# Re-ordering the first chunk of a fused LayerNorm, linear attention and gated-MLP kernel: half-chunk first units, K inside gate/up, LayerNorm further ahead, weight loads in thirds

## Chip, cores, metric

The kernel runs on one core of a Trainium2 chip. The metric is the device time of one execution in microseconds (us), lower is better. A time is a median of several executions; the span in a profile is about 1.7 us shorter than the time of that same execution (566.5 and 568.19 us before, 536.1 and 537.85 changed).

## The reference

One block of a model, on 2048 tokens of width 576 in bf16. A LayerNorm feeds two branches that are added to the input: linear attention with 32 heads of 18, and a gated MLP of width 4608.

```python
xn = layernorm(x)                                  # x: 1 x 2048 x 576
q, k, v = heads(xn @ wqkv)
pq, pk = phi(q), phi(k)                            # phi(t) = (t + 1 if t > 0 else exp(t)) + 1e-6
kv = einsum("bhsd,bhse->bhde", pk, v);  z = sum_s pk
attn = (pq @ kv / (pq . z + 1e-6)) @ wo
mlp = (sigmoid(xn @ w_gate) * (xn @ w_up)) @ w_down
out = x + attn + mlp
```

## The kernel before

Tokens are worked on in 16 tiles of 128 and in 4 chunks of 512 (four tiles). What matters here:

- *GU(c, f)*: one of 36 gate/up units of a chunk: 9 x 2 matmuls of 64 rows, the upper and the lower half of the array at the same time, into a pair of accumulator banks. Then tanh on ScalarE and one VectorE operation that writes hT.
- *K(t)*: the K projection of two tiles, one in each half of the array; it takes two pairs of banks. *K1(t)* is the same for one tile. Its output goes through exp (ScalarE) and two VectorE operations into pk.
- *L1, L2, L3a, L3b, TD*: LayerNorm statistics (VectorE), small powers and products (POOL), normalisation (ScalarE for tiles 4 and up), then the transposed copy xs by two DMA transposes per tile, issued on SP's queue.
- *Q*: query projections. *G*: products xn by pk over all 16 tiles. They need all of K. *den*: denominators, whose reciprocals take VectorE 3.3 us each.
- *ring*: three weight slots of four units each, gate in partitions 0 to 63, up in 64 to 127.
- *pair()* hands out one of four pairs of banks.

A small scheduler derives semaphore waits from the named tiles; each engine executes its instructions in program order. The start and the first chunk are:

```python
TP(0) ...                                  # tiles 0-3: transposed on TensorE
K1(0); TP(2) ...; K1(1); TP(3) ...; K1(2); K1(3)
LNx(4)                                     # normalise and transpose tiles 4, 5
ring_load(1, sp)                           # slot 1, issued behind those transposes
f = 0
for p, nf in enumerate((5, 3, 3, 3, 2, 2)):
    ta = 6 + 2 * p
    for n in range(nf):
        GU(0, f); f += 1
        ...                                # statistics of ta, ta+1; LNx(ta); x loads; slot 2
    K(4 + 2 * p)                           # needs the transposes issued one round before
...                                        # [cut: Q, G(4), z]
G(0); dq = den(0, (0, 1)); G(1)
for fn in dq: fn()                         # two reciprocals at once
...                                        # [cut: same for den 2, 3 and 4; rest of gate/up with Q]
attn(0, a0); finish(0, a0)
for fn in dq: fn()                         # two reciprocals ahead of ...
attn(1, a1); finish(1, a1)                 # ... what frees the accumulator
```

## Time and profile before

| | before |
|---|---|
| median time | 569.01 us (568.57 to 569.63, 3 runs) |
| span of the profiled run | 566.5 us |
| first Q unit, which needs all K, begins | 97.53 us |
| chunk 0 ends (chunk 1's gate/up begins) | 228.69 us |
| chunks 1 and 2 | 112.14 us each |

These are lines of the profile page: the engines' busy time (part 1), and the granted clock in 40 slices of 14 us, in tenths (part 2).

```profile
PE 525.4 (93%) x4615; PEld 318.1 (56%) x4615; DVE 258.7 (46%) x365; ACT 128.4 (23%) x212; POOL 36.0 (6%) x65
...
PEclk9969797998999979999999999999999999999999
```

TensorE is 93% busy, but the clock line shows that part of that is at a lower clock, always in the first 16 slices (the granted clock was 0.50, half, from 32 to 40 us). The next lines are from the view of waits, TensorE alone: who waited for whom, us in total, times, longest.

```profile
PE ps L478 <- DMA xs<-wd: 10.9, 3, 5.5
PE ps L513 <- DMA ring<-in_B_w_gate_dram: 9.2, 1, 9.2
PE ps L532 <- DVE ost L707: 7.4, 3, 6.4
...
PE ps L492 <- DVE den L541: 2.5, 1, 2.5
```

The first two are waits for transposed tiles and for weights, the last two for a VectorE that is busy with reciprocals. All but 1 us of these four waits lie before 229 us.

### The profile page before, as it was taken

Reading aid. Unit: us, or ns where it says so; the run is one execution under the profiler, and the core shown is the slowest. Engines: PE = TensorE matmul, PEld = TensorE weight load, DVE = VectorE, ACT = ScalarE, POOL = GpSimd, SP = SyncE. Lnnn points to the kernel's source line nnn. Section 1 sums busy time; section 2 is a strip of 40 time slices with the busy share of each in tenths; the row PEclk is TensorE's granted clock in tenths of the full one; section 3 lists DMA queues with packets and bytes.
Section 4 is the critical chain, followed back from the end, with each engine's and each line's share of the span. In section 5 each row is a group of like instructions: output and inputs, shape, how many; then the busy total and the mean of one; then the engine's idle time right before and its main releaser. Section 6 shows DMA issues by size and latency. Waiting matters only on the chain.

```text
span 566.5 us, 10534 instructions
## 1 busy us (share of the span) xinstructions
PE 525.4 (93%) x4615; PEld 318.1 (56%) x4615; DVE 258.7 (46%) x365; ACT 128.4 (23%) x212; POOL 36.0 (6%) x65
## 2 busy tenths in 40 slices
PE   7739668998999959999999999999999999999997
PEld 3416457864546737444447774444477744444776
DVE  5606362798642097233338903333388033333001
ACT  4504233312432100232230002232200022233000
POOL 3504242300000000000000000000000000000000
PEclk9969797998999979999999999999999999999999
DMA  9299984428848010277774103667831047760000
GB/s 248 58 216 229 150 166 89 119 61 254 195 101 184 6 42 22 61 145 153 168 162 91 43 22 83 146 141 155 168 84 43 23 100 146 148 130 1 22 22 21
DMA packets 72999, 62.54 MB, mean 110 GB/s; under 512 B 17786, under 2 KB 72954, under 8 KB 72954
## 3 DMA queue, kind: packets, MB, share of 16 engines
q1 hardware_dynamic: 52202, 41.08, 32.0%
q10 hardware_dynamic: 20752, 20.79, 18.1%
q8 instruction: 36, 0.59, 0.5%
q14 instruction: 9, 0.07, 0.1%
HBM read 55.97 MB, written 2.36 MB: 103 GB/s over the span
## 4 chain that ended last, share of the span: by engine, by line
PE 82%; DVE 9%; DMA 5%; issue 1%; ACT 1%; POOL 1%; SPq 1%; DVEq 0%; ACTq 0%
PE ps L513 47%; PE ps L693 22%; DVE den L549 5%; PE ps L492 4%; PE ps L701 3%; PE ps L478 3%; PE ps L560 2%; DMA xs<-wd 2%; DMA ring<-in_B_w_up_dram 2%; DVE den L541 1%; DMA pqT<-in_A_x_dram 1%; PE ps L532 1%; PE ps L467 1%; DVE stats L387 1%; DVE ost L707 1%
## 5 line engine op out<-in xcount | busy, mean ns | idle before, releaser
L513 PE MATMUL ps<-xs,ring 64*128 64x512 bf16 x2592 | 286.6, 378 | 11.5 <-DMA ring<-in_B_w_gate_dram 9.2
L513 PEld LDWEIGHTS ps<-xs,ring 64*128 64x128 bf16 x2592 | 133.9, 95 | 159.6 <-issue 15.2
L521 DVE SCALAR_TENSOR_TENSOR hT<-tg,ps 128x512 bf16<-128x512 f32 x144 | 98.9, 687 | 167.9 <-PE ps L513 143.9
L519 ACT ACTIVATE tg<-ps 128x512 f32<-128x512 f32 x144 | 85.9, 597 | 320.8 <-PE ps L513 303.2
L693 PE MATMUL ps<-wd,hT 128*128 128x288 bf16 x1152 | 147.1, 287 | 0.0
L693 PEld LDWEIGHTS ps<-wd,hT 128*128 128x128 bf16 x1152 | 112.9, 98 | 32.1 <-issue 2.2
L549 DVE RECIPROCAL den<-den 126x512 f32<-126x512 f32 (+1 forms) x20 | 66.9, 3343 | 0.0
L707 DVE SCALAR_TENSOR_TENSOR ost<-ps,xr 128x576 bf16<-128x576 f32 x16 | 12.1, 756 | 78.7 <-PE ps L701 72.7
L478 PE MATMUL ps<-hT,xs 64*128 64x288 bf16 x216 | 19.7, 335 | 11.9 <-DMA xs<-wd 10.9
L452 DVE TENSOR_SCALAR et<-et 128x576 bf16<-128x576 bf16 (+2 forms) x36 | 11.9, 331 | 34.1 <-ACT et L451 34.1
L451 ACT ACTIVATE et<-ps 128x576 bf16<-128x576 f32 (+2 forms) x36 | 20.6, 616 | 30.3 <-PE ps L492 16.4
L492 PE MATMUL ps<-xs,wqM 64*126 64x512 bf16 (+1 forms) x180 | 22.4, 397 | 2.5 <-DVE den L541 2.5
L478 PEld LDWEIGHTS ps<-hT,xs 64*128 64x128 bf16 x216 | 15.0, 110 | 16.2 <-issue 10.9
L701 PE MATMUL ps<-wqM,pqT 126*128 126x288 bf16 (+1 forms) x160 | 22.1, 286 | 0.0
L460 POOL TENSOR_TENSOR hT<-hT,wd 128x576 f32<-128x576 f32 x15 | 19.2, 1281 | 38.3 <-DVE wd L453 37.7
L492 PEld LDWEIGHTS ps<-xs,wqM 64*126 64x126 bf16 (+1 forms) x180 | 14.7, 137 | 9.1 <-DVE den L541 3.0
L541 DVE TENSOR_SCALAR den<-ps 126x512 f32<-126x512 f32 (+1 forms) x20 | 13.0, 684 | 14.8 <-PE ps L532 14.8
L701 PEld LDWEIGHTS ps<-wqM,pqT 126*128 126x128 bf16 (+1 forms) x160 | 15.6, 98 | 4.0
L560 PE MATMUL ps<-wd 128*128 128x288 bf16 x128 | 16.3, 286 | 0.0
L387 DVE BATCH_NORM_STATS2 stats<-pqT 128x6 f32<-128x288 bf16 x32 | 14.6, 456 | 3.7 <-DMA pqT<-in_A_x_dram 3.2
L560 PEld LDWEIGHTS ps<-wd 128*128 128x128 bf16 x128 | 12.4, 98 | 3.5
L550 DVE TENSOR_TENSOR pqT<-pqT,den 126x512 bf16<-126x512 bf16 (+1 forms) x20 | 13.8, 691 | 0.7
(49 smaller groups left out, 117.5 us busy)
## 6 DMA issues: line engine op xcount, KB each, us to landing
ring<-in_B_w_gate_dram SPq DMA_DIRECT2D x36, 576.0 KB, 5.6
ring<-in_B_w_up_dram ACTq DMA_DIRECT2D x33, 576.0 KB, 7.9
wd<-in_B_w_down_dram SPq DMA_DIRECT2D x2, 1296.0 KB, 6.5
wd<-in_B_w_down_dram SPq DMA_DIRECT2D x2, 1152.0 KB, 7.2
xr<-in_A_x_dram SPq DMA_DIRECT2D x16, 144.0 KB, 2.3
out_dram<-ost SPq DMA_DIRECT2D x16, 144.0 KB, 1.8
ring<-in_B_w_up_dram SPq DMA_DIRECT2D x3, 576.0 KB, 9.9
hT<-in_A_wqkv_dram ACTq DMA_DIRECT2D x2, 576.0 KB, 6.5
```

The lines of the kernel that those rows point to most:

```text
L387: V(lambda e, h=h: e.bn_stats(stats_t[:, so + 6 * h:so + 6 * h + 6], x_in(t, 288 * h, 288)), reads=["x[%d]" % t], writes=["st%d" % (t % 4)])
L451: A(lambda e: e.activation(e3, src, AF.Exp), reads=kb, writes=["et%d" % j])
L460: P(lambda e: e.tensor_tensor(zacc, zacc, pk(tt, 0, _D), ALU.add), reads=["pk[%d]" % tt, "zacc"], writes=["zacc"])
L478: T(lambda e, s=s, h=h, p0=p0, tt=tt, b=b: e.matmul(bank(b + h, 128, 0, 288), xs(s, 128 * tt, 128, p0, p0 + 64), wk(s, 288 * h, 288, p0, p ...
L492: T(lambda e, k=k, half=half, c=c, i=i, g=g, sl=sl, p0=p0: e.matmul(bank(b + half, g, 0, _CH), wq(k, i, half, g), xs(sl, _CH * c, _CH, p0, ...
L513: T(lambda e, k=k, half=half, sl=sl, p0=p0: e.matmul(bank(b + half), ring(r, k, fo, half), xs(sl, _CH * c, _CH, p0, p0 + 64), start=(k == ...
L519: A(lambda e: e.activation(tg, bank(b), AF.Tanh, scale=0.5), reads=["pb%d" % b], writes=["tg%d" % sj])
L521: V(lambda e: e.scalar_tensor_tensor(hT(f), tg, 1.0, bank(b + 1), ALU.add, ALU.mult), reads=["pb%d" % (b + 1), "tg%d" % sj], writes=["hT[% ...
L549: V(lambda e: e.reciprocal(dn(j, g), dn(j, g)), reads=["dn%d" % j], writes=["dn%d" % j])
L560: T(lambda e, t=t, h=h: e.matmul(bank(b + h, 128, 0, 288), xn(t, 128 * j, 128), pk(t, 288 * h, 288), start=(t == 0), stop=(t == NT - 1)), ...
L693: T(lambda e, f=f, h=h: e.matmul(bank(acc + h, 128, 0, 288), hT(f, 128 * st, 128), wd(f, h), start=(f == 0), stop=False), reads=["hT[%d]" ...
L701: T(lambda e, i=i, g=g, h=h: e.matmul(bank(acc + h, 128, 0, 288), pqT(i, 128 * t, 128, g), M(i, h, g), start=False, stop=(i == _NG - 1)), ...
```

## The change

The intent is to give TensorE gate/up work as soon as two tiles are transposed, to keep K out of the start, to have LayerNorm's output ready earlier, and to remove the waits for reciprocals. Its core, cut:

```diff
+        x_load(1, 2, (), act)
+        x_load(2, 4)
+        ring_mixed(0, act)              # slot 0 before the K weights, in thirds of 192 KB
 ...
+        ring_mixed(1)                   # slots 1 and 2 at the start, thirds gate/up alternating
+        ring_mixed(2)
 ...
+        GU_mm(0, 0, b0, 0, 256)         # units 0 and 1 on tiles 0 and 1
+        GU_mm(0, 1, b1, 0, 256)
 ...                                     # tiles 2 and 3
+        GU_mm(0, 0, b0, 256, 256); GU_out(0, 0, b0)
+        GU_mm(0, 1, b1, 256, 256); GU_out(0, 1, b1)
 ...
-        for p, nf in enumerate((5, 3, 3, 3, 2, 2)):
+        late = {4: lambda: (x_load(8, 12), ring_mixed(3)), 6: lambda: x_load(12, 16), 8: lambda: ring_mixed(4),
+                10: wq_load, 12: lambda: ring_mixed(5)}
+        kt = {3: 0, 5: 2, 8: 4, 10: 6, 12: 8, 14: 10, 16: 12, 17: 14}
+        for f in range(2, FK):
+            GU(0, f)
+            ta = f + 2 - f % 2
+            if f < 14:
+                if f % 2 == 0: LNa(ta)                 # statistics
+                else: LNb(ta); late.get(ta, ...)()     # normalise, transpose; loads
+            if f in kt: K(kt[f])
 ...
-        G(0); dq = den(0, (0, 1)); G(1); (both reciprocals)
+        dq = den(0, (0, 1)); G(0); dq[0](); G(1); dq[1]()
 ...
-                for fn in dq:
-                    fn()
                 attn(1, a1)
                 finish(1, a1)
+                for fn in dq:
+                    fn()
 ...
-  plan = {0: [(8, (0, 1)), (24, (2, 3))], 1: [(8, (4,))]}
+  plan = {0: [(8, (0, 1))], 1: [(8, (2, 3))], 2: [(8, (4,))]}
```

Cut here: `pair()` now gives the pair that was given or released longest ago, tiles 1 and 3 are partly copied out by VectorE, and the loads of w_down are spread over units 19 to 25. The four K1 become two K, and the dummy matmuls (`warm`) at the start are placed differently. `plan` says in which tile of the down projection, and after how many of its steps, the dens of the next chunk are placed.

More of the change, by code (lines that the diff above doesn't have):

```diff
@@ L223, in bass_parallel_sum__linear_attn_block__glu_gated_glu__prompt_kernel, with release @@
         held = set()
-        turn = [0]
+        order = [0, 1, 2, 3]
         def pair():
-            while True:
-                p = turn[0] % 4
-                turn[0] += 1
-                if p not in held:
-                    return 2 * p
+            p = next(q for q in order if q not in held)
+            order.remove(p)
+            order.append(p)
+            return 2 * p
+        def release(b):
+            p = b // 2
+            held.discard(p)
+            order.remove(p)
+            order.append(p)
         def xs(slot, c0, n, p0=0, p1=128):
@@ L300, in ring, with x_load @@
             return ring_t[64 * half:64 * half + 64, o:o + 128]
-        def x_load(ta, tb, extra=()):
+        def x_load(ta, tb, extra=(), q=None):
             dst = pqT_t[:, ta * _D:tb * _D].rearrange("p (t d) -> p t d", t=tb - ta)
-            load("x%d" % ta, dst, xv[:, ta:tb, :], ["x[%d]" % t for t in range(ta, tb)], None, extra)
+            load("x%d" % ta, dst, xv[:, ta:tb, :], ["x[%d]" % t for t in range(ta, tb)], q, extra)
         wg_v = B_w_gate.rearrange("(k p) f -> p k f", p=64)
@@ L307, in bass_parallel_sum__linear_attn_block__glu_gated_glu__prompt_kernel, with ring_part @@
         wu_v = B_w_up.rearrange("(k p) f -> p k f", p=64)
-        ringL_p = [dprod("rl%d" % r) for r in range(R)]
-        ringU_p = [dprod("ru%d" % r) for r in range(R)]
+        KP = ((0, 3), (3, 6), (6, 9))
+        ringL_p = [[dprod("rl%d%d" % (r, n)) for n in range(3)] for r in range(R)]
+        ringU_p = [[dprod("ru%d%d" % (r, n)) for n in range(3)] for r in range(R)]
         WS = 128 * _FS
-        def ring_load(u, qu=None, extra=()):
+        def ring_part(u, up, n0, n1, q, extra=()):
@@ L313, in ring_load @@
             r = u % R
             j = u % NSLOT
-            dl = ring_t[0:64, r * 9 * WS:(r + 1) * 9 * WS].rearrange("p (k w) -> p k w", k=9)
-            du = ring_t[64:128, r * 9 * WS:(r + 1) * 9 * WS].rearrange("p (k w) -> p k w", k=9)
-            sl = wg_v[:, :, j * WS:(j + 1) * WS]
-            su = wu_v[:, :, j * WS:(j + 1) * WS]
-            sch.dma(sp, ringL_p[r], lambda e: e.dma_start(dl, sl), writes=["ringL[%d]" % r], extra=extra)
-            sch.dma(qu or act, ringU_p[r], lambda e: e.dma_start(du, su), writes=["ringU[%d]" % r], extra=extra)
+            k0, k1 = KP[n0][0], KP[n1 - 1][1]
@@ new lines, in ring_part, with ring_load @@
+            p0 = 64 if up else 0
+            dst = ring_t[p0:p0 + 64, (r * 9 + k0) * WS:(r * 9 + k1) * WS].rearrange("p (k w) -> p k w", k=k1 - k0)
+            src = (wu_v if up else wg_v)[:, k0:k1, j * WS:(j + 1) * WS]
+            name = "ringU" if up else "ringL"
+            sch.dma(q, (ringU_p if up else ringL_p)[r][n0], lambda e: e.dma_start(dst, src),
+                    writes=["%s[%d]%d" % (name, r, n) for n in range(n0, n1)], extra=extra)
+        def ring_load(u):
+            ring_part(u, 0, 0, 3, sp)
+            ring_part(u, 1, 0, 3, act)
@@ L322, in bass_parallel_sum__linear_attn_block__glu_gated_glu__prompt_kernel, with ring_mixed @@
+        def ring_mixed(u, qu=None, extra=()):
+            for n in range(3):
+                ring_part(u, 0, n, n + 1, sp, extra)
+                ring_part(u, 1, n, n + 1, qu or sp, extra)
         x_load(0, 1)
+        x_load(1, 2, (), act)
+        x_load(2, 4)
+        ring_mixed(0, act)
         wkv = A_wqkv[:, _KOFF:_KOFF + _D]
@@ L332, in bass_parallel_sum__linear_attn_block__glu_gated_glu__prompt_kernel @@
         load("wk3", wk_dst(5, 4), wkv[64:576, :].rearrange("(k p) c -> p k c", p=128), ["wk3"], act)
-        x_load(1, 2)
-        x_load(2, 4)
         x_load(4, 6)
-        ring_load(0, sp)
         x_load(6, 8)
+        ring_mixed(1)
+        ring_mixed(2)
         def wq_load():
@@ L358, in bass_parallel_sum__linear_attn_block__glu_gated_glu__prompt_kernel, with wd_load @@
         _nwd = [0]
-        def wd_load(f0, f1, alias=()):
+        def wd_load(f0, f1, extra=()):
             pr = dprod("wd%d" % _nwd[0])
@@ L364, in wd_load @@
             src = B_w_down[f0 * 128:f1 * 128, :].rearrange("(f p) c -> p f c", p=128)
-            sch.dma(sp, pr, lambda e: e.dma_start(dst, src), writes=["wdf[%d]" % f for f in range(f0, f1)] + list(alias))
+            sch.dma(sp, pr, lambda e: e.dma_start(dst, src), writes=["wdf[%d]" % f for f in range(f0, f1)], extra=extra)
         P = lambda fn, reads=(), writes=(): sch.op(pool, fn, reads, writes)
@@ L420, in bass_parallel_sum__linear_attn_block__glu_gated_glu__prompt_kernel, with TP @@
         xs3 = xs_t[:, :].rearrange("p (s c) -> p s c", c=S)
-        def TP(t):
+        def TP(t, ea, eb):
             b = pair()
-            for s in (0, 1, 2, 3, 5, 6, 7, 8, 4):
+            for s in (5, 6, 7, 8, 0, 1, 2, 3, 4):
                 c0 = 128 * s if s < 5 else 64 + 128 * (s - 5)
@@ L429, in TP @@
                   reads=["xn[%d]" % t] + (["xw[%d]" % t] if s == 4 else []) + ["ident"], writes=["pb%d" % bb])
-            A(lambda e: e.activation(xs3[:, 0:5, 128 * t:128 * t + 128], bank_bf(b, 640).rearrange("p (s c) -> p s c", c=128), AF.Identity),
-              reads=["pb%d" % b], writes=["xsA[%d]" % t])
-            A(lambda e: e.activation(xs3[:, 5:9, 128 * t:128 * t + 128], bank_bf(b + 1, 512).rearrange("p (s c) -> p s c", c=128), AF.Identity),
-              reads=["pb%d" % (b + 1)], writes=["xsB[%d]" % t])
+            for st, bb, s0, n, nm in ((eb, b + 1, 5, 4, "xsB[%d]"), (ea, b, 0, 5, "xsA[%d]")):
+                dst, src = xs3[:, s0:s0 + n, 128 * t:128 * t + 128], bank_bf(bb, 128 * n).rearrange("p (s c) -> p s c", c=128)
+                if st is act:
+                    A(lambda e, dst=dst, src=src: e.activation(dst, src, AF.Identity), reads=["pb%d" % bb], writes=[nm % t])
+                else:
+                    V(lambda e, dst=dst, src=src: e.tensor_copy(dst, src), reads=["pb%d" % bb], writes=[nm % t])
         def TD(t):
@@ L460, in K_out @@
                 P(lambda e: e.tensor_tensor(zacc, zacc, pk(tt, 0, _D), ALU.add), reads=["pk[%d]" % tt, "zacc"], writes=["zacc"])
-        def K1(t):
-            b = pair()
-            for s in range(5):
-                rows = 128 if s < 4 else 64
-                for h in range(2):
-                    T(lambda e, s=s, h=h, rows=rows: e.matmul(bank(b + h, 128, 0, 288), xs(s, 128 * t, 128, 0, rows), wk(s, 288 * h, 288, 0, rows),
-                                                              start=(s == 0), stop=(s == 4)),
-                      reads=["xsA[%d]" % t] + (["wk0"] if s < 4 else ["wk1"]), writes=["pb%d" % (b + h)])
-            K_out(t, b)
         def K(t):
@@ L501, in bass_parallel_sum__linear_attn_block__glu_gated_glu__prompt_kernel, with GU_mm @@
         endA = [[]]
-        def GU(c, f):
-            u = c * NSLOT + f // _FS
-            r = u % R
+        def GU_mm(c, f, b, c0, n):
+            r = (c * NSLOT + f // _FS) % R
             fo = (f % _FS) * 128
-            b = pair()
-            xr_ = xsr(range(c * TPC, (c + 1) * TPC))
+            t0 = (_CH * c + c0) // 128
+            xr_ = xsr(range(t0, t0 + n // 128))
             for k in range(9):
@@ L513, in GU, with GU_out @@
                     T(lambda e, k=k, half=half, sl=sl, p0=p0: e.matmul(
-                        bank(b + half), ring(r, k, fo, half), xs(sl, _CH * c, _CH, p0, p0 + 64),
+                        bank(b + half, 128, c0, n), ring(r, k, fo, half), xs(sl, _CH * c + c0, n, p0, p0 + 64),
                         start=(k == 0), stop=(k == 8), tile_position=(p0, 0)),
-                      reads=[("ringU[%d]" if half else "ringL[%d]") % r] + xr_, writes=["pb%d" % (b + half)])
+                      reads=[("ringU[%d]%d" if half else "ringL[%d]%d") % (r, k // 3)] + xr_, writes=["pb%d" % (b + half)])
+        def GU_out(c, f, b):
+            u = c * NSLOT + f // _FS
             sj = f % 2
@@ L522, in GU @@
               reads=["pb%d" % (b + 1), "tg%d" % sj], writes=["hT[%d]" % f] + al)
+            if c == 0 and f < FK:
+                return
             if f % _FS == _FS - 1 and u + R < NUSE:
                 ring_load(u + R)
+        def GU(c, f):
+            b = pair()
+            GU_mm(c, f, b, 0, _CH)
+            GU_out(c, f, b)
         _jd = [0]
@@ L573, in G @@
                       reads=["pb%d" % (b + h)], writes=["GT[4]"])
+        m3 = lambda t_: t_[0:_GW, 0:_GW].rearrange("p (b r) -> p b r", r=_DH)
         warm(11, 7)
@@ L577, in bass_parallel_sum__linear_attn_block__glu_gated_glu__prompt_kernel @@
         L2(0, 1)
-        L1(1, (0,))
+        L1(1)
+        L2(1, 1)
         L3v(0)
-        m3 = lambda t_: t_[0:_GW, 0:_GW].rearrange("p (b r) -> p b r", r=_DH)
-        TP(0)
-        L1(1, (1, 2))
-        L2(1, 1)
+        TP(0, act, act)
         L1(2, (0,))
         L3v(1)
-        warm(3, 7)
-        TP(1)
+        warm(1, 7)
+        TP(1, dve, act)
         L1(2, (1, 2))
         L2(2, 1)
-        L1(3, (0,))
-        L3v(2)
-        K1(0)
-        TP(2)
-        L1(3, (1, 2))
-        L2(3, 1)
-        L1(4)
-        L3v(3)
-        K1(1)
-        TP(3)
+        b0, b1 = pair(), pair()
+        warm(2, 7)
+        GU_mm(0, 0, b0, 0, 256)
+        GU_mm(0, 1, b1, 0, 256)
+        L1(3)
+        L2(3, 1)
+        L3v(2)
+        TP(2, act, act)
+        L3v(3)
+        TP(3, dve, act)
+        GU_mm(0, 0, b0, 256, 256)
+        GU_out(0, 0, b0)
+        GU_mm(0, 1, b1, 256, 256)
+        GU_out(0, 1, b1)
         P(lambda e: e.affine_select(m3(mtmp_t), m3(ones_t), pattern=[[-_DH, 7], [0, _DH]], compare_op=ALU.is_ge,
@@ L603, in bass_parallel_sum__linear_attn_block__glu_gated_glu__prompt_kernel, with LNa, LNb @@
                                     fill=0.0, base=_DH - 1, channel_multiplier=-1), reads=["mtmp"], writes=["mask"])
-        L1(5)
-        L2(4, 2)
-        L3a(4, 2)
-        K1(2)
-        K1(3)
-        def LNx(ta):
+        def LNa(ta):
+            L1(ta)
+            L1(ta + 1)
+            L2(ta, 2)
+            L3a(ta, 2)
+        def LNb(ta):
             for t in (ta, ta + 1):
@@ L613, in LNx @@
                 TD(t)
-        LNx(4)
-        ring_load(1, sp)
-        f = 0
-        for p, nf in enumerate((5, 3, 3, 3, 2, 2)):
-            ta = 6 + 2 * p
-            for n in range(nf):
-                GU(0, f)
-                f += 1
-                if n == 0 and p < 2:
-                    x_load(8 + 4 * p, 12 + 4 * p, paced())
-                if ta < NT:
-                    if n == 0:
-                        L1(ta)
-                    if n == 1:
-                        L1(ta + 1)
-                        L2(ta, 2)
-                        L3a(ta, 2)
-                        if nf == 2:
-                            LNx(ta)
-                    if n == 2:
-                        LNx(ta)
-                if p == 0 and n == 2:
-                    ring_load(2, sp, paced())
-                if p == 2 and n == 0:
-                    wq_load()
-            K(4 + 2 * p)
+        late = {4: lambda: (x_load(8, 12), ring_mixed(3)), 6: lambda: x_load(12, 16), 8: lambda: ring_mixed(4),
[5 more added lines that the diff above has]
+            if f < 14:
+                if f % 2 == 0:
+                    LNa(ta)
+                else:
+                    LNb(ta)
+                    late.get(ta, lambda: None)()
+            if f in kt:
+                K(kt[f])
         wv_load()
         wd_load(34, NF)
+        ring_mixed(6)
         Q(((0, 0), (0, 2)))
@@ L659, in bass_parallel_sum__linear_attn_block__glu_gated_glu__prompt_kernel @@
               reads=["pb%d" % zb, "mask"], writes=["Zx[%d]" % i])
+        dq = den(0, (0, 1))
         G(0)
-        dq = den(0, (0, 1))
+        dq[0]()
         G(1)
-        for fn in dq:
-            fn()
+        dq[1]()
         dq = den(0, (2, 3))
         G(2)
-        for fn in dq:
-            fn()
+        dq[0]()
+        G(3)
+        dq[1]()
         dq = den(0, (4,))
-        G(3)
-        for (f0, f1) in ((0, 9), (9, 18), (18, 26), (26, 34)):
-            wd_load(f0, f1, ["pk[%d]" % t for t in range(NT)] + ["xn[%d]" % t for t in range(NT)] + ["xw[%d]" % t for t in range(NT)])
+        free = paced()
+        wds = [(0, 9), (9, 18), (18, 26), (26, 34)]
         qs = [((1, 0), (1, 2)), ((1, 1), (1, 3)), ((2, 0), (2, 2)), ((2, 1), (2, 3)), ((2, 4), (3, 4)), ((3, 0), (3, 2)), ((3, 1), (3, 3))]
@@ L676, in bass_parallel_sum__linear_attn_block__glu_gated_glu__prompt_kernel @@
             GU(0, f)
-            if dq:
-                dq.pop(0)()
-            elif qs:
+            if f % 2 == 1 and wds:
+                wd_load(*wds.pop(0), extra=free)
+            if f == FK + 1:
+                dq[0]()
+            if f >= FK + 3 and f % 2 == 1 and qs:
                 Q(qs.pop(0))
@@ L710, in finish @@
             sch.dma(sp, out_p[j], lambda e: e.dma_start(out2d[128 * t:128 * t + 128, :], ost_t[:, j * _D:(j + 1) * _D]), reads=["ost%d" % j])
-            held.discard(acc // 2)
+            release(acc)
             if t + 2 < NT:
@@ L772, in bass_parallel_sum__linear_attn_block__glu_gated_glu__prompt_kernel @@
                 finish(0, a0)
+                attn(1, a1)
+                finish(1, a1)
                 for fn in dq:
                     fn()
-                attn(1, a1)
-                finish(1, a1)
                 tiles = (2, 3)
-                plan = {2: [(8, (2, 3)), (24, (4,))]}
+                plan = {2: [(24, (2, 3))], 3: [(24, (4,))]}
             else:
@@ L782, in bass_parallel_sum__linear_attn_block__glu_gated_glu__prompt_kernel @@
                 tiles = range(TPC)
-                plan = {0: [(8, (0, 1)), (24, (2, 3))], 1: [(8, (4,))]} if c + 1 < NCH else {}
+                plan = {0: [(8, (0, 1))], 1: [(8, (2, 3))], 2: [(8, (4,))]} if c + 1 < NCH else {}
             for st in tiles:
```

## The prediction

> **What bounds the kernel now.** I read the chain of work that ended last first. It is 82% TensorE, but the rest is what a reordering can win, so I read the chain in order of time. Three gaps carry most of it: weights (27.87), transposed tiles (57.45 and 81.03), and reciprocals (199.25).
>
> ```profile
> 18.09 4.76 PE ps L513 x44
> 25.80 1.27 SPq L439
> 27.87 9.93 DMA ring<-in_B_w_up_dram
> 37.94 3.45 PE ps L513 x17
> ...
> 57.45 5.76 DMA xs<-wd
> 63.34 4.48 PE ps L478 x35
> ...
> 81.03 5.49 DMA xs<-wd
> 86.77 4.47 PE ps L478 x35
> ```
>
> L513 is gate/up (GU), L478 a pair of K projections. Columns are start, length and what. The first line below, from the timeline of the same stretch, is K with a warm clock: 2.44 us busy, 2.2 from start to the next group, against 4.48 above. The others, from the chain restricted to the end of chunk 0, are the reciprocals.
>
> ```profile
> 73.61 2.47 PE L478 MATMUL ps<-hT,xs 64*128 64x288 bf16 x36
> ...
> 199.25 3.27 DVE den L549
> 202.52 0.02 issue
> 202.54 0.69 DVE pqT L550
> 203.24 3.27 DVE den L549
> 206.51 0.02 issue
> 206.53 0.03 DVE pqT L550
> 206.56 0.57 issue
> 207.14 0.76 DVE ost L707
> 207.90 0.04 issue
> 207.94 1.11 PE ps L532 x2
> ```
>
> Then the table by stretches (PE, PEld, DVE, ACT, POOL, clock, DMA share, GB/s).
>
> ```profile
> 30.00:40.00 10.00, 2.65 (x11) 0.96 (x13) 0.00 (x0) 0.00 (x0) 0.00 (x0) 0.53 1.15 235
> 60.00:70.00 10.00, 7.05 (x57) 5.24 (x59) 1.60 (x4) 2.89 (x5) 1.54 (x6) 0.66 0.94 164
> 80.00:90.00 10.00, 3.51 (x29) 2.51 (x31) 3.65 (x10) 2.17 (x3) 3.50 (x7) 0.76 1.00 183
> 260.00:566.00 306.00, 302.28 (x2650) 177.19 (x2646) 118.57 (x135) 55.49 (x93) 0.00 (x0) 1.00 0.43 93
> ```
>
> After 260 us TensorE is busy 302 of 306 us: nothing is left there. Chunks 1 to 3 cost 112.14 us each (starts 228.69, 340.82, 452.96). All that can be won lies before 228.7. From the chain, with a full clock, one GU is 1.945 us (180 matmuls in 19.43 are ten of them), a K pair 2.19, a tile of the down projection 8.82 plus 1.23 for attention. Chunk 0 holds 36 GU (70.0), K (17.5 as eight pairs), 10 Q units (19.4), G (18.0), four down tiles (40.2) and about 5 of small things: 170 us. It takes 228.7, so some 58 us are start, waits and half clock.
>
> **What the Trainium skill says.** "TensorE: Matmul & The Clock Gate", Part 1 (the HAM clock gate): the array falls to half clock after an idle window of some microseconds and needs a busy one to recover. The trace agrees: clock 0.53 after the 10 us wait, and K at 4.48 instead of 2.2. A removed wait therefore returns more than itself. The same page's specification table calls the ScalarE and VectorE queues strict FIFO; the trace agrees at 207.14, where the cheap ost operation, needed to free the accumulator, stands behind two reciprocals. "DMA: Bandwidth & Descriptors", Issuing engines are not separate DMA queues: splitting loads over SP and ACT saves issue time, not bandwidth. The trace agrees: with both queues loaded, 30 to 36 us shows a DMA share of 1.1 and only 217 to 223 GB/s.
>
> **The change, part by part.** I place the start of the first Q unit, 97.53 us now.
>
> (1) Start. x tiles 0 to 3 and weight slot 0 go first, so tiles 0 and 1 are transposed by 9 us (today TP0 starts at 6.73 and TP1 at 8.56, plus evacuation). Bytes by then: x 0.59 MB and slot 0 1.18 MB, which at the 283 to 383 GB/s of 2 to 8 us takes 6 us from about 2 us on, with some competition from wk. Two half units run from 9.5 to 11.5 (9 x 2 x 256 columns are half of 1.945 each). Tiles 2 and 3 come at 14, because VectorE does two statistics blocks, a copy and two normalisations between. Then the other halves (to 16), units 2 and 3 (19.9), K(0) at about 20. Today GU begins at 17.7 and stalls from 25.9 to 37.9.
>
> (2) Weights. Bytes still to load after slot 0 are wk rest 1.1, x4 to x7 0.59, slots 1 and 2 2.36: 4.05 MB at 225 GB/s is 18 us, done at 27.5. Slot 1 is needed at 22, with thirds arriving first; slot 2 after 30. The 12 us weight stall goes.
>
> (3) Steady stretch. From f=2 to f=17 TensorE wants 16 x 1.945 + 8 x 2.19 = 48.6 us, so from 16.0 the bare end is 64.7. That is 33 us better than 97.5, but the other engines bind. VectorE per two GU, one K pair and one LayerNorm pair is 2 x 0.60 + 2 x 1.02 + (4 x 0.48 + 2 x 0.21 + 0.18) = 5.8 us against TensorE's 6.08. Worse, there is a loop in program order: statistics on VectorE, then 1.57 to L3b's start (49.92 to 51.49 now, through POOL), L3b 1.62 on ACT, tanh 0.60 behind it, hT 0.60, then the next statistics, 2.3. That sums to 6.7 us. In the two rounds where K's exp also sits in that loop it is nearly 9. Rounds of 8.9, 8.8, 6.6, 6.7 and 6.7 carry the statistics of pair 4 (19.4) to those of pair 14 at 57.2; three more K pairs and the remaining GU then end at 74, not 64.7.
>
> (4) SP's queue. It issues, in order, 24 DMA transposes, 18 thirds, x and wq between pairs. Transposes take 1.25 us to issue when quiet, but 4.61, 2.17, 2.23 and 1.27 behind a weight backlog at 29 us. I estimate six pairs at 7.2, 7.8, 5.5, 6.3, 5.9, 6.5 = 39 us, 18 thirds at 0.45 (less than the 0.65 of a whole half slot) = 8, x and wq 3.6. From 25 us that is 76, and with the 4.2 median to landing K(14) can begin near 79 if it never waits for input, 75 if contention is mild. K(14) cold costs 2.2 more. So Q begins between 74 and 84; I take 79.5. That is 18 us won here of 33.
>
> (5) Q to the end of chunk 0's GU (97.53 to 176.21 = 78.7 now). Needed: 3 Q 5.83, G(4) 2.3, z 0.55, five den 1.1, four G 15.7, 18 GU and 7 Q 48.6 = 74.1. The wait of TensorE for den (2.50 at 127) and the half-clock unit after it (3.70 for 1.94) go, since reciprocals are spread. New: the first den now stands before G(0), so it waits for Zx, which today ended its first two pieces about 1.1 us after the z matmuls. 75.2, so 3.5 won.
>
> (6) The down tail of chunk 0 (52.5 now). finish(1) moves ahead of its reciprocals: the 6.37 us wait for ost and the slow matmuls after it (5.19 for 32, against 3.92) go. 8.3 won, 44.2 remain. VectorE has 8 us reciprocals during the next tile, which takes 10 us: they fit.
>
> (7) Chunks 1 and 2: each shows one 0.5 us wait for ost at the last den. Spreading over three tiles wins about 1.5 in all.
>
> Sum: 79.5 + 75.2 + 44.2 + (566.5 - 228.7 - 1.5 = 336.3) = 535.2 of span. Times are 2.5 above the span now (569.01 to 566.5), so 537.7; I say 538.
>
> **Rivals.** (a) *TensorE bound throughout*: the LayerNorm loop is absorbed by the four accumulator pairs. Then Q starts at 65 to 67 and the time is 523 to 526. For it: three rounds at 6.7 are only 10% over 6.08. Against: a K pair needs two accumulator pairs at once, so the slack is about one GU. (b) *ACT/VectorE loop binds, SP doesn't*: Q at 74, time 532. For it: SP issues at 1.25 quiet. (c) *SP's transposes take the place of the weight wait*: Q at 84 with K(14) cold, time 542 or a little more. For it: 29 to 40 us now; against: less weight traffic coincides with the later pairs. (d) *Early weights come late*: the backlog of ring thirds delays wk or slot 1 by 3 to 6 us. This adds only in part, because pair 4's loop starts after K(0): 540 to 545. (e) No gain, as the removed wait reappears in full: I see no mechanism, since 12 us of (6) and (5) don't touch LayerNorm at all.
>
> **Range and chances.** (b), (c) and their middle take most of the weight; (a) perhaps 12%, (d) or something unseen 12%. I put 538 with 528 to 547. Faster by over 2% means under 557.6: that needs only (5), (6) and a small half of (3), so 0.97.
>
> **What would show it.** Q's first matmul (today's L492) at 75 to 84; gate/up starting at 9 to 11 and no long wait for ring; DMA xs<-wd still a wait ahead of the last K pairs if (c), waits of K and GU on hT or pk (VectorE) if (b), and none if (a). In SP's own queue, transposes of 1.2 to 2.3 us, issued nearly back to back. Chunk 0's tail near 44 us with no wait on ost; chunks of 111.4. VectorE over 80% busy from 20 to 60 us. I am wrong if Q starts outside 72 to 86, if GU's start slips beyond 13 us because slot 0 lands late, or if the reciprocals moved behind finish(1) come back as a wait at the start of chunk 1.

## The result

The changed kernel takes 537.97 us (median of 4, 537.76 to 539.44) against 568.94 for the kernel before in the same rounds. The ratio is 0.946, with a 95% interval of 0.944 to 0.948. Ratios here are the mean time of one kernel's fast runs over that of the other's in the same rounds, so not quite the ratio of the medians. Later runs used other rounds, where the kernel before had medians of 566.6 to 568.1 us, so experiments are compared by their ratio to it and by the times inside their traces.

The same lines of the page, changed kernel:

```profile
PE 518.2 (97%) x4683; PEld 317.0 (59%) x4683; DVE 259.5 (48%) x367; ACT 126.0 (24%) x210; POOL 35.8 (7%) x65
...
PEclk9998989999999999999999999999999999999999
```

TensorE does nearly the same work in 7 us less busy time. Less of it is at half clock: the mean granted clock was 0.970 before and is 0.994 now; two slices still dip, to 8. (Line numbers moved: L522 is now gate/up, L488 K, L502 Q, L551 den, L707 the down projection, L721 the last sum.) TensorE's waits in the changed kernel:

```profile
PE ps L488 <- DMA xs<-wd: 3.9, 3, 1.6
PE ps L488 <- DVE wd L473: 3.1, 4, 1.3
...
PE ps L522 <- DVE wd L473: 1.4, 1, 1.4
...
PE ps L551 <- DVE Zexp L670: 1.0, 1, 1.0
```

The wait for weights (9.2 and 2.3 us before) is gone, so are the waits for ost and for reciprocals. What is left is three short waits for transposes, waits for VectorE to empty K's accumulators (pk lies in wd), and the wait for Zx that the prediction had announced. By stages, with the prediction beside it:

| stage | before | predicted | measured |
|---|---|---|---|
| start to first Q | 97.5 | 79.5 | 80.0 |
| Q to the end of chunk 0's gate/up | 78.7 | 75.2 | 75.6 |
| down projection of chunk 0 | 52.5 | 44.2 | 44.1 |
| the rest | 337.8 | 336.3 | 336.3 |
| span | 566.5 | 535.2 | 536.1 |

The loop that the prediction names is seen in VectorE's and ScalarE's timelines. In one round, after statistics that began at 36.77: normalisation, then tanh behind it, then hT, then the next statistics (start, us, operation):

```profile
40.63 1.62 ACT L434 ACTIVATE wd<-pqT,nm,rs 128x576 bf16<-128x576 bf16 x2 [5.01 <-POOL nm L430]
...
42.16 0.57 ACT L531 ACTIVATE tg<-ps 128x512 f32<-128x512 f32 x1
...
42.77 0.69 DVE L533 SCALAR_TENSOR_TENSOR hT<-tg,ps 128x512 bf16<-128x512 f32 x1 [2.94 <-ACT tg L531]
...
43.37 0.95 DVE L405 BATCH_NORM_STATS2 stats<-pqT 128x6 f32<-128x288 bf16 x2
```

In the down tail of chunk 0, the den that stood 6.37 us before now follows without a gap in the chain, after a piece that ends at 184.88:

```profile
184.88 0.43 PE ps L551 x2
185.31 2.94 PE ps L707 x24
```

The chain of waits in time order just before Q shows what set its start:

```profile
63.43 5.54 DMA xs<-wd
...
69.22 2.29 PE ps L488 x34
...
73.93 2.35 DMA xs<-wd
...
76.52 3.70 PE ps L488 x34
```

K(12) waits for the transposes of tile 13, then K(14) for those of tile 15, and K(14) runs near half clock (granted 0.58), 3.70 us where K(12) took 2.29. In SP's queue at that time (start, us, operation):

```profile
64.75 0.60 SPq L326 DMA_DIRECT2D ring<-in_B_w_gate_dram  x1
...
68.89 0.61 SPq L326 DMA_DIRECT2D ring<-in_B_w_up_dram  x1
69.62 1.21 SPq L458 DMA_TRANSPOSE xs<-wd  x1
...
73.93 1.20 SPq L459 DMA_TRANSPOSE xs<-wd  x1
```

The six thirds of weight slot 5 stand ahead of the last transposes. They were issued from 64.75 to 69.50; slot 5 is first used by unit 20, which starts at about 111 us, some 40 us later. The transposes behind them took only 1.20 to 1.27 us each to issue, so it was the place in the queue that held them here.

### The profile page after: what moved, and what is told of

Its sections match the earlier page's. It is cut to its first block, busy times and chain, and to the rows that moved or that the text cites. A ratio compares the mean times of both kernels' runs of the same rounds, so it can differ in the third digit from the quotient of the medians.

```text
span 536.1 us, 10699 instructions
## 1 busy us (share of the span) xinstructions
PE 518.2 (97%) x4683; PEld 317.0 (59%) x4683; DVE 259.5 (48%) x367; ACT 126.0 (24%) x210; POOL 35.8 (7%) x65
## 3 DMA queue, kind: packets, MB, share of 16 engines
q10 hardware_dynamic: 19152, 19.17, 17.5%
## 4 chain that ended last, share of the span: by engine, by line
PE 90%; DVE 4%; DMA 3%; SPq 1%; ACT 1%; issue 1%; POOL 0%; DVEq 0%; ACTq 0%
PE ps L522 50%; PE ps L707 26%; PE ps L715 4%; PE ps L488 3%; PE ps L579 3%; PE ps L502 3%; DMA xs<-wd 1%; DMA ring<-in_B_w_gate_dram 1%; DVE wd L473 1%; PE ps L551 1%; DVE et L472 1%; DVE pqT L473 1%; DVE stats L405 1%; SPq L458 0%; DVE hT L533 0%
## 5 line engine op out<-in xcount | busy, mean ns | idle before, releaser
L522 PE MATMUL ps<-xs,ring 64*128 64x512 bf16 (+1 forms) x2628 | 285.9, 373 | 4.1 <-DVE wd L473 1.4
L522 PEld LDWEIGHTS ps<-xs,ring 64*128 64x128 bf16 x2628 | 134.9, 94 | 150.1 <-DVE xs L453 1.9
L707 PE MATMUL ps<-wd,hT 128*128 128x288 bf16 x1152 | 145.8, 286 | 0.0
L707 PEld LDWEIGHTS ps<-wd,hT 128*128 128x128 bf16 x1152 | 112.2, 98 | 31.2 <-issue 1.7
L721 DVE SCALAR_TENSOR_TENSOR ost<-ps,xr 128x576 bf16<-128x576 f32 x16 | 12.1, 758 | 73.6 <-PE ps L715 54.9
L488 PE MATMUL ps<-hT,xs 64*128 64x288 bf16 x288 | 23.3, 308 | 7.0 <-DMA xs<-wd 3.9
L488 PEld LDWEIGHTS ps<-hT,xs 64*128 64x128 bf16 x288 | 17.0, 102 | 13.3 <-DVE wd L473 3.5
L502 PE MATMUL ps<-xs,wqM 64*126 64x512 bf16 (+1 forms) x180 | 20.8, 376 | 0.0
L502 PEld LDWEIGHTS ps<-xs,wqM 64*126 64x126 bf16 (+1 forms) x180 | 14.1, 128 | 5.5
L579 PEld LDWEIGHTS ps<-wd 128*128 128x128 bf16 x128 | 12.5, 98 | 3.4
```

The costliest lines, as they stand in the source:

```text
L488: T(lambda e, s=s, h=h, p0=p0, tt=tt, b=b: e.matmul(bank(b + h, 128, 0, 288), xs(s, 128 * tt, 128, p0, p0 + 64), wk(s, 288 * h, 288, p0, p ...
L502: T(lambda e, k=k, half=half, c=c, i=i, g=g, sl=sl, p0=p0: e.matmul(bank(b + half, g, 0, _CH), wq(k, i, half, g), xs(sl, _CH * c, _CH, p0, ...
L522: T(lambda e, k=k, half=half, sl=sl, p0=p0: e.matmul(bank(b + half, 128, c0, n), ring(r, k, fo, half), xs(sl, _CH * c + c0, n, p0, p0 + 64 ...
L579: T(lambda e, t=t, h=h: e.matmul(bank(b + h, 128, 0, 288), xn(t, 128 * j, 128), pk(t, 288 * h, 288), start=(t == 0), stop=(t == NT - 1)), ...
L707: T(lambda e, f=f, h=h: e.matmul(bank(acc + h, 128, 0, 288), hT(f, 128 * st, 128), wd(f, h), start=(f == 0), stop=False), reads=["hT[%d]" ...
```

## The experiments

The prediction named two mechanisms for the stretch from 20 to 80 us: a loop through VectorE, POOL and ScalarE, and SP's queue. Theory 1 said that the queue set Q's start. Its rival, theory 2, said that the loop did. Each edit is against the changed kernel unless said otherwise.

| run | time, median | ratio to before, 95% | Q begins |
|---|---|---|---|
| changed kernel | 537.97 | 0.9460 (0.944 to 0.948) | 80.0 |
| a_whole_late | 536.28 | 0.9452 (0.940 to 0.950) | 77.6 |
| b_slot5_last | 532.86 | 0.9389 (0.935 to 0.943) | 75.4 |
| c_norm_behind | 539.83 | 0.9499 (0.945 to 0.955) | 83.2 |
| d_abc | 534.24 | 0.9411 (0.937 to 0.945) | 75.4 |
| o_slots_on_act | 538.66 | 0.9486 (0.946 to 0.952) | 81.1 |
| n_act_behind | 539.23 | 0.9482 (0.944 to 0.952) | 81.3 |
| b_den_after | 533.12 | 0.9384 (0.936 to 0.941) | 75.8 |
| p_behind_x_early | 533.55 | 0.9391 (0.937 to 0.942) | 77.7 |
| h_units_whole | 541.99 | 0.9544 (0.952 to 0.957) | 84.0 |
| l_norm_later | 541.91 | 0.9543 (0.952 to 0.957) | 85.1 |
| e_tail_only (edit of before) | 555.32 | 0.9786 (0.976 to 0.981) | 97.3 |
| g_finish_first (edit of before) | 558.65 | 0.9835 (0.981 to 0.986) | 97.1 |

All gave correct results.

### Fewer issues on SP: a_whole_late

```diff
+        def ring_whole(u):
+            ring_part(u, 0, 0, 3, sp)
+            ring_part(u, 1, 0, 3, sp)
-  ring_mixed(3), ring_mixed(4), ring_mixed(5), ring_mixed(6)
+  ring_whole(3), ring_whole(4), ring_whole(5), ring_whole(6)
```

> The changed kernel with weight slots 3 to 6 loaded as two DMAs each on SP instead of six thirds. Theory 1 (SP's queue of issues binds from 24 to 75 us): each slot costs SP 1.3 us instead of 3.9, so the transposes of tiles 14 and 15, issued from 69.6 in the changed kernel, can go as soon as their input is ready at 63.5; the waits of K(12) (1.2) and K(14) (1.1 and 1.6) and the half-clock K(14) (3.7 against 2.2) go, Q begins near 75 instead of 80.0, time 532.5 to 534. Theory 2 (the loop VectorE, POOL, ScalarE binds and the queue only fills what is idle): under 1 us, 537 to 538.

The ratio is 0.945, not distinguishable from the changed kernel; Q begins 2.5 us earlier, half of what theory 1 expected. SP's queue shows why:

```profile
64.22 0.60 SPq L326 DMA_DIRECT2D ring<-in_B_w_gate_dram  x1
64.87 0.64 SPq L326 DMA_DIRECT2D ring<-in_B_w_up_dram  x1
65.61 1.96 SPq L458 DMA_TRANSPOSE xs<-wd  x1
...
69.32 3.30 SPq L458 DMA_TRANSPOSE xs<-wd  x1
```

The last transposes were issued 4 us earlier, but they now took 1.3 to 3.3 us each to issue instead of 1.2, while 1.18 MB of weights were under way. A load of 576 KB took as long to issue as a third of it (0.60 against 0.61). So of 4 us freed in the queue only 1.1 reached K(14), which began at 75.46 instead of 76.52; the other 1.4 us is that K(14) then ran at full clock (2.29). The number of issues alone is not what holds the transposes, and theory 1's 532.5 to 534 us were not reached.

### The same loads later: b_slot5_last

```diff
-  late = {..., 12: lambda: ring_mixed(5)}
+  late = {..., 14: lambda: ring_mixed(5)}
```

> The changed kernel with the six thirds of weight slot 5 issued after the transposes of tiles 14 and 15 instead of before them; nothing else. Theory 1 (SP's issues bind): those transposes start near 64.8 instead of 69.6 and K(14) begins near 74 with a warm clock, Q near 76.2; 3.5 to 4 us less, 534 to 534.5. Theory 2 (VectorE, POOL, ScalarE loop binds): no change within 0.5 us, about 538.

Q begins at 75.4 and the ratio is 0.939, 0.7% below the changed kernel's, in a separate session. This is a little more than theory 1 expected (76.2): K(14) begins 3.3 us earlier, and its warm clock gives 1.3. No wait for transposes remains in TensorE's list. The waits left before Q are for VectorE and ScalarE, all but one of them before 48 us. After that TensorE stops once, for the longest of them:

```profile
PE ps L488 <- DVE hT L533: 1.4, 1, 1.4
```

### The loop relieved: c_norm_behind

```diff
-                if f % 2 == 0: LNa(ta)
-                else: LNb(ta); late.get(ta, ...)()
+            if f % 2 == 0 and f <= 14:
+                if f > 2: LNb(f); late.get(f, ...)()   # a unit later: behind its tanh
+                if f < 14: LNa(ta)
```

> The changed kernel with the two normalisations of a pair moved behind the tanh of the next unit in ScalarE's order (and their transposes with them), so that tanh no longer waits for POOL's work on that pair. Theory 1 (SP binds): the waits of TensorE for pk and hT between 26 and 48 us shrink from 5.9 us to under 3, but the transposes start 1 to 2 us later and Q begins at the same time or up to 1.5 us later: 538 to 539.5. Theory 2 (the loop binds): Q 3 to 5 us earlier, 533 to 535.

The ratio, 0.950, is a little above what theory 1 expected (538 to 539.5 us, 0.946 to 0.948), though its interval is wide, and Q is 3.2 us later where at most 1.5 was expected. The waits for pk fell from 4.5 us (3.1 + 1.4) to 1.2. But TensorE stood 3.4 us for hT at 37 us: the unit's VectorE operation was behind the statistics of tiles 8 and 9, whose x had been asked for later. The waits for transposes, which now begin 3 us later (27.5 instead of 24.4), grew from 3.9 to 6.9. So this order wins nothing. It is no clean test of theory 2, since it brought a new wait for VectorE and moved the transposes.

### All three: d_abc

The edits of a, b and c together.

> All three together: late slots as two DMAs, slot 5 behind the last transposes, normalisation behind the next tanh. Theory 1 alone right: as a_whole_late, 532.5 to 534, since the loop is no bound. Both queue and loop are bounds, one hidden behind the other (what I hold): the gains exceed either alone, Q near 70 to 72, 528 to 530.5.

Q begins at 75.4, exactly as in b. I had held that the gains would exceed either alone; they did not, and the time is just above what was named for theory 1 alone (532.5 to 534). The 3.2 us wait for hT at 37 us was still there, so this is no clean test either.

### Is it the queue? o_slots_on_act

```diff
-  late = {4: lambda: (x_load(8, 12), ring_mixed(3)), 6: ..., 8: lambda: ring_mixed(4), 10: wq_load, 12: lambda: ring_mixed(5)}
+  late = {4: lambda: x_load(8, 12), 6: ..., 10: wq_load}
+  on_act = {6: 3, 9: 4, 14: 5}       # after these units, gate and up whole, on ScalarE's queue
```

> The changed kernel with weight slots 3, 4 and 5 issued whole from ScalarE's queue after units 6, 9 and 14, so that no weight load stands ahead of a transpose in SP's queue; all else as changed. The runs so far suggest that it is the bytes ahead of the transposes, not SP's time per issue, that delayed the last two pairs (whole slots on SP won little, moving slot 5 behind won 5 us). Theory 1b (bytes ahead in the same queue): as b_slot5_last, Q begins at 75 to 76, the loop of VectorE, POOL and ScalarE being next; ratio to before 0.937 to 0.941. Rival (all transfers share the 16 engines, so the queue does not matter): transposes as slow as now, ratio 0.945 to 0.948.

Theory 1b, that the bytes must be ahead in the same queue, fell. The ratio is 0.949, no better than the changed kernel. The chain before K(12):

```profile
62.40 10.73 DMA xs<-wd
73.14 0.24 issue
73.38 3.80 PE ps L488 x35
```

Slot 5 was issued at 60.5 on the other queue, beside the transposes of tiles 12 and 13. The last of these then took 10.7 us to land, against 5.5 in the changed kernel. So weights under way at the same time hold up a transpose from the other queue too. (The loads here are also whole, and slot 5 comes 4 us earlier than in the changed kernel; the run does not separate that.) That the 16 engines are shared is what the Trainium skill says ("DMA: Bandwidth & Descriptors", Issuing engines are not separate DMA queues); here it is seen as a transpose that lands twice as late.

### Both relieved, weights on the other queue: n_act_behind

The edit of o, with that of c, and x tiles 8 to 11 loaded before slot 2.

> The same, with the normalisations behind the next tanh (as in c_norm_behind) and x tiles 8 to 11 loaded before slot 2, 12 to 15 behind the transposes of tiles 4 and 5 (in c_norm_behind TensorE stood 3.4 us for the statistics of tiles 8 and 9, whose x had come late). If two bounds lie one behind the other, both are now away: K(14) can begin near 66 to 70, Q at 68 to 72, ratio 0.926 to 0.933. If the loop was never a bound: as o_slots_on_act.

The waits for pk and the 3.4 us wait for hT are gone, as intended: no wait of TensorE for pk is listed. In their place stand three waits for transposes, 12.4 us in all, the two longest 5.2 and 5.9 us. Q begins at 81.3 and not at 68 to 72. By its time alone this is the outcome named for a loop that was never a bound; the trace shows more: the loop's waits can be removed, but then the transfers take over at once.

### Two attempts to beat b: b_den_after and p_behind_x_early

```diff
-        dq = den(0, (0, 1)); G(0); dq[0]()
+        G(0); dq = den(0, (0, 1)); dq[0]()        # both runs, on top of b
```

> b_slot5_last with the first den of chunk 0 back behind G(0): its wait for Zx (0.98 us in the changed kernel) is covered by G(0) as in the kernel before. By part 5 of the prediction about 1.0 us less than b_slot5_last's 0.939: ratio 0.936 to 0.938, no wait of L551 for Zx left. If the reciprocals, now 4 us later, hold a later unit instead: no gain, and a wait of GU or Q for hT or den near 107 to 115 us.

The 1 us wait for Zx is gone, but unit 21 now waits 0.56 us at 107.5 for the accumulator of the last den, since all reciprocals are 4 us later. From Q to the end of gate/up it is 75.3 us instead of 75.6. The ratio, 0.938, cannot be told from b's.

> b_den_after with the normalisations behind the next tanh and x tiles 8 to 11 loaded before slot 2. Of the two bounds found, the loop is relieved by the order (n_act_behind had no wait for pk or tanh left) and slot 5 no longer competes with the last transposes. If the transfers before Q (about 1.1 of 16 engines' time from 30 to 72 us) are now the bound: Q at 72 to 75.5, ratio 0.931 to 0.937. If the loop was what held b_slot5_last: Q at 68 to 70, ratio 0.925 to 0.93.

Here the normalisations are also behind the next tanh and x tiles 8 to 11 come early. Waits for pk fell to 1.1 us, waits for transposes rose to 7.7, Q begins at 77.7, and the ratio is again 0.939. Its transposes begin at 27.4 instead of 24.8. This is the outcome named for transfers as the bound, with Q some 2 us later than the range that I had set and the ratio just above its range (0.931 to 0.937).

### One part undone: h_units_whole

```diff
-        GU_mm(0, 0, b0, 0, 256); GU_mm(0, 1, b1, 0, 256)       # after tile 1
-        GU_mm(0, 0, b0, 256, 256) ... GU_mm(0, 1, b1, 256, 256)
+        GU_mm(0, 0, b0, 0, _CH) ... GU_mm(0, 1, b1, 0, _CH)    # after tile 3
```

> The changed kernel with units 0 and 1 whole after tile 3 instead of half after tile 1. By part 1 of the prediction TensorE does 1.96 us of gate/up work later and everything from unit 2 on moves by that: 1.5 to 2.5 us slower, ratio 0.948 to 0.951. If the stretch to Q is bound by SP and transfers that do not depend on units 0 and 1: no difference, 0.946.

The span grew by 4.9 us (536.1 to 541.0), twice what was expected. TensorE's timeline gives the missing part:

```profile
11.44 1.53 PE L446 MATMUL ps<-ident,wd 128*128 128x128 bf16 x18 [2.67 <-DVE wd L422]
13.69 9.63 PE L522 MATMUL ps<-xs,ring 64*128 64x512 bf16 x72 [0.71 <-ACT xs L451]
```

Without the half units TensorE stands 2.67 us, and the granted clock was 0.60 from 13.7 to 18 us. Four units took 9.63 us where 4 x 1.945 = 7.78 would be a full clock. The half units are 2 us of work and also what kept the clock up here: the four executions of this run have a mean granted clock of 0.986 to 0.987, those of the changed kernel 0.989 to 0.994. Everything after them moved by some 3 us, and the last K pair and Q then ran at half clock for part of the time, which gives the rest.

### LayerNorm a round later: l_norm_later

```diff
-            ta = f + 2 - f % 2; if f < 14: LNa(ta) / LNb(ta)
+            if 4 <= f < 16: LNa(f) / LNb(f - 1)
```

> The changed kernel with each LayerNorm pair one round (two units) later, so not a pair further ahead, K where it is. Transposes begin 6 to 9 us later and every K pair from K(4) on waits for them; if that stretch is bound by them as the prediction says, Q moves from 80 to 86 to 89: ratio 0.957 to 0.963. If the time ahead is not needed: 0.946 to 0.95.

Q begins at 85.1 instead of 80.0, a little less than expected; the ratio is 0.954. Four waits for transposes, 8.3 us in all, and four K pairs near half clock (3.85 to 4.03 us; two in the changed kernel). The time ahead is worth 5 us, clock included, and it is needed by the transposes. The loads that hang on these rounds move with them.

### The parts after Q, put into the kernel before: e_tail_only and g_finish_first

e_tail_only takes the new order of den and reciprocals, finish(1) first, one den per tile, and the spread loads of w_down and Q units. g_finish_first takes only this:

```diff
-                for fn in dq:
-                    fn()
                 attn(1, a1)
                 finish(1, a1)
+                for fn in dq:
+                    fn()
```

> The kernel before with only the parts of the change that lie after the first Q unit: the first den before G(0) and reciprocals spread, finish(1) before its reciprocals, dens one per tile. By the prediction's parts 5, 6 and 7: 3.5 + 8.3 + 1.5 = 13.3 us less, ratio 0.976 to 0.978. If the parts do not add up, the head of the kernel hides or needs some of it: ratio above 0.98.

> The kernel before with four lines exchanged: attn(1) and finish(1) before the two reciprocals. By part 6 of the prediction 8.3 us less (6.4 of wait, about 1.9 of half clock), ratio 0.985 to 0.987. Rival: the wait turns up again at the next den, since its reciprocals are now 8 us later; ratio above 0.99.

e won 12.0 us by medians (567.3 to 555.32), against 13.3 expected; its ratio, 0.9786, lies just outside the expected range, with an interval that covers most of it. From Q to the end of gate/up its trace has 75.6 us, and 44.1 for the down projection, the same as in the changed kernel: the tail does not depend on the head. g won 8.65 by medians; its down projection of chunk 0 takes 44.1 us too, and the rival's wait at the next den is not in its list; the ratio, 0.9835, is a little better than expected. So four exchanged lines are more than a quarter of the whole gain.

## Why the prediction was right

Both signs that it had named for its rivals are in the changed kernel's trace: waits for transposes before the last K pairs (c), and waits for pk and hT (b). So the outcome is between the two, as said. By its own steps:

- **Part 1, the start: right.** Gate/up begins at 9.02 (9.5 foretold), the second halves at 13.6 (14), K(0) at 19.8 (20). What it did not say, and h_units_whole shows, is that the half units are worth 4.9 us: 2 us as work, the rest from a clock that dropped without them and what followed from that.
- **Part 2, weights: right.** No wait of gate/up for weights is in the list. (Four of the later traces have one of 0.3 to 0.6 us at 10 us, so slot 0 comes just in time.) No run put the slots back, so this piece is read from the two traces alone.
- **Part 3, the loop: right in size.** The statistics of the six pairs were foretold to begin at 19.4, then after rounds of 8.9, 8.8, 6.6, 6.7 and 6.7. Measured, from VectorE's timeline: 19.38, 28.06, 36.77, 43.37, 50.00, 57.12, so rounds of 8.7, 8.7, 6.6, 6.6 and 7.1. With the transfers out of the way, b_slot5_last came to 532.9 us, near rival (b)'s 532, and the waits left in its trace are those of the loop's engines. That fits a loop that binds; it is not shown by a run, since each run that removed the loop's waits also brought waits for transposes. Wrong was "VectorE over 80% busy from 20 to 60 us": it was 27.4 of 40 us, 69%. A loop can bind though none of its engines is full.
- **Part 4, SP's queue: the sum right by luck, the reason half right.** From the first transpose's issue at 24.44 to the end of the last at 75.13 are 50.7 us; the estimate was 50.6. But with the small gaps between issues, transposes took 33 us instead of 39 (they were mostly quiet), the 18 thirds took 12.5 us instead of 8 (0.61 each, one of 1.49), and the queue stood idle for about 2 us: errors that cancelled. That the issues ahead held the last transposes is what the changed kernel shows: from 59.5 to 75.1 us the queue issued almost without a pause. Slow transposes behind a backlog were a term of the estimate; a and o show that they are also a second bound right behind the queue, for with issues taken away transposes were slow beside weights under way, from the same queue (a) or the other (o). Taking the loads out of that stretch removes both; b shows that this is worth 4.6 us of Q's start. The half-clock K(14) was foretold at 2.2 us extra and cost 1.4.
- **Part 5: right.** 75.6 against 75.2, with the announced wait for Zx at 0.99. It was not worth avoiding: b_den_after won 0.3.
- **Part 6: right.** 44.1 against 44.2, and g shows it alone.
- **Part 7: right.** Chunk 1 runs from 199.75 to 311.19, 111.44 us, against 111.4.

The head won 17.5 us at Q's start (97.5 to 80.0), the tail about 13, as foretold (18 and 13.3). That the totals agree so closely is partly luck: 79.5 was picked inside a range of 74 to 84, and the prediction added 2.5 us from span to time by subtracting the span of one execution from the median of others, where the difference within an execution is 1.7. The span came out 0.9 us above the foretold one, and this made up for it. Two of its readings are slightly off: the warm K that it shows is 2.47 us busy, not 2.44, and its clock of 0.53 is a slice that holds most of the wait itself (0.58 in the 3.5 us after it). The best version found is b_slot5_last, at 532.9 us and 0.939; b_den_after cannot be told from it.

Open: two bounds of nearly equal length lie one behind the other before Q. By the waits in their traces b is held by the loop, p by the transfers, and no order tried frees both at once. What the early slots 1 and 2, the thirds at the start, K in pairs, the new order of pair() and VectorE's share of the copies are worth by themselves was not tested; the traces say only that a third and a whole half slot take the same time to issue.

## What to carry over

When a stretch mixes work from several engines, write the loop that runs through them in program order and add its measured pieces: it can set the pace at 70% busy. A load that nobody needs soon should not be under way while something that is needed now is, and putting it in another queue did not help here. Ahead of a long, unhurried operation (here a reciprocal), look for a short one whose result frees a buffer.

## What the Trainium skill lacked or had wrong

- "DMA: Bandwidth & Descriptors", Rules for kernel authors: "A transpose next to ordinary DMAs needs nothing". That holds for correctness in these runs, but the page does not say what ordinary DMAs beside it cost it in time. Here a transpose took 1.2 to 1.3 us to issue when quiet and up to 4.95 us beside weight loads (o_slots_on_act), and one landed 10.7 us after its issue.
- The same page does not say how the time to issue a load changes with its size. Here it did not fall with it: 0.61 us for 192 KB and 0.60 to 0.64 for 576 KB. Cutting loads into thirds cost three times the issue time.
- "TensorE: Matmul & The Clock Gate", Why this matters for your kernels, warns of idle gaps above some 3 us between bursts of matmuls. As a measure for one gap this held in neither direction here. Shorter gaps were followed by a low clock: one of 2.50 us in the kernel before (granted clock 0.57 just after), one of 2.08 in l_norm_later (0.60), one of 2.67 in h_units_whole, with transposes and then a 0.71 us wait after it (0.60). Longer ones were not: 3.45 us in c_norm_behind and 3.24 in d_abc (1.00 after both). Two waits of 1.26 and 0.75 us with one matmul between them were followed by 0.61 in the changed kernel, and waits of 1.27 and 0.74 by 1.00 in a_whole_late. So the length of a gap alone does not tell, and which K pair runs at half clock can differ between two such kernels.
